# Attention means of two heads interleaved by 16 rows, fewer matmuls for v means and gate logits, and a new order of the work

## The chip, the cores and the metric

The kernel runs on one core of one Trainium2 chip. The metric is the device time of one execution in microseconds (us), as the median of several executions. A separate execution is recorded by the hardware profiler; it runs somewhat longer than the timed ones. PE is TensorE (PEld its weight loads), DVE is VectorE, ACT is ScalarE, POOL is GpSimd, SP issues DMAs.

## The reference, cut to what matters

Attention over 8 batches x 8 heads, 576 rows of 64, in two branches: a coarse one on means of 4 rows (144 x 144), repeated 4 times, and a local one over 7 neighbours. The sum, as 4608 rows of 512, goes through a top-1 mixture of 8 experts.

```python
q_d = q.reshape(B, H, Sd, 4, D).mean(axis=3)      # k_d, v_d alike; Sd = 144, D = 64
out_d = sm_attn(q_d, k_d, v_d)                    # softmax(q_d k_d^T / 8) v_d
out_up = np.repeat(out_d, 4, axis=2)
mask = np.abs(pos[:, None] - pos[None, :]) < 4
out_local = softmax(where(mask, q k^T / 8, -1e9)) @ v
attn_out = out_up + out_local                     # then x = (4608, 512)

logits = x @ w_gate                               # 8 experts
e_idx = np.argmax(logits, axis=1)
gate_w = softmax(logits)[e_idx];  eom = sigmoid(x @ w_output_gate)
out[mask_e] = gate_w * eom[:, e] * (relu(x[mask_e] @ w1[e]) @ w2[e])
```

## The kernel before

The work is cut into tasks, each on one engine with an assumed cost, a priority, inputs, and buffers that it takes and gives. A list scheduler inside the program orders them once, when the program is built; on the chip each engine runs its tasks in that fixed order. A unit `u` is one batch and two heads (32 units); heads 0 and 1 lie on partitions 0 to 63 and 64 to 127.

```python
def cast(u, i):                                   # i = 0: q, 1: k
    nc.gpsimd.tensor_copy(t16..., d["f", i])      # 96 x 768, f32 -> f16

def turn(u):                                      # 12 transposes into PSUM, tag "S"
    for i in range(2):
        for m in range(6):
            nc.tensor.transpose(tf[:, i, :]..., t16[:, m, :], id16[0:96, 0:96])

def turned(u):   nc.scalar.copy(d["qkT"]..., d["t"]...)
def qk_means(u): nc.vector.tensor_reduce(d["qkd"], d["qkT"]...(r=4), op=ALU.add)

def v_means(u):
    d["pd"] = pd = psA.tile([128, 2, 512], F32, tag="S", name="pd", bufs=3)
    for w in range(NW):                           # NW = 10 windows of 57 rows
        for h in range(2):
            j, c = (w // 2, 0) if w < 8 else (2 * h + 1, D)
            nc.tensor.matmul(pd[32 * j:32 * j + 32, h, c:c + D], lhsT=pv[64 * h:64 * h + 64, w, :],
                             rhs=d["v"][64 * h:64 * h + 64, w, 0:D], start=(w % 2 == 0), stop=(w % 2 == 1), ...)

def vd_out(u):                                    # three copies PSUM -> SBUF
    nc.scalar.copy(t[:, 0:2, 0:D], d["pd"][:, :, 0:D])
    for h in range(2):
        r = slice(64 * h + 32, 64 * h + 64)
        nc.scalar.copy(t[r, 2, 0:D], d["pd"][r, h, D:2 * D])

def scores(u):                                    # f16
    for g in range(2):                            # the mask is added by a matmul with the identity
        nc.tensor.matmul(ps[:, g, 0:NL], lhsT=id16, rhs=mk[:, g, :], start=True, stop=False, ...)
    for j in range(4):
        for h, r in hs:
            mm(ps[32 * j:32 * j + 32, h, MC:NH], kd[r, MW[2 * j]:MW[2 * j] + 32], qd[r])
    for w in range(NW):
        for h, r in hs:
            mm(ps[r, w // 5, LC[w]:LC[w] + QN[w]], d["qkT"][r, S + KW[w]:S + KW[w] + 64], qT[r, Q0[w]:Q0[w] + QN[w]])
    for g in range(2):
        for h, r in hs:
            mm(ps[r, g, TC:MC], kd[r, SD - 64:SD], qd[r, NK * g:NK * g + NK])

def exps(u):
    nc.scalar.activation(e[:, :, TC:NH], d["ps"][:, :, TC:NH], AF.Exp, scale=scale / 16.0)
    nc.scalar.activation(e[:, :, 0:TC], d["ps"][:, :, 0:TC], AF.Exp, scale=scale)

def values(u):                                    # f32
    for t in range(NB):                           # 5 blocks x 2 windows x 2 heads
        ... nc.tensor.matmul(po[h][64 * a:64 * a + 64, t, :], lhsT=e[r, w // 5, LC[w]:LC[w] + 64], rhs=t_v[r, w, 0:65], ...)
    for g in range(2):
        for h in range(2):
            nc.tensor.matmul(po[h][0:NK, NB + g, :], lhsT=e[:, h, MC + NK * g:MC + NK * g + NK], rhs=t_vd[:, h, 0:65], ...)
    for g in range(2):
        for h in range(2):
            r = slice(64 * h + 32, 64 * h + 64)
            nc.tensor.matmul(po[h][0:NK, NB + g, :], lhsT=e[r, g, TC:MC], rhs=t_vd[r, 2, 0:65], ...)
# ... norm (DVE), then per batch: upsample (PE), x_sum (DVE), x_high (ACT), x_low (POOL), x_turn (PE), x_turned ...

def logits(b, ts):                                # gate logits of one block of 128 rows
    for i, t in enumerate(ts):
        ms = [(xT[:, x + c, :], wg[:, c, y:y + 2 * E]) for x, y in ((0, 0), (0, 2 * E), (4, 0)) for c in range(4)]
        for j, (a, m) in enumerate(ms):
            nc.tensor.matmul(lg[:, i, :], lhsT=a, rhs=m, start=(j == 0), stop=(j == 11))

def logits_out(b, ts): nc.scalar.copy(lg_s[n][:, c:c + len(ts), :], lg[:, 0:len(ts)])

XT_ACT = (1, 3)                                   # blocks whose transposed copy is ACT's; the others are DVE's
# buffers: three large PSUM tiles "S" (tqk, pd, ps, po, pu, py), two small "T" (us, tp, lg, rk, ...)
```

After the routing come the experts: the rows of each are fetched, `up` (PE, pu) with a relu on ACT and DVE, `down` (PE, py), `weigh` (ACT) and `put` (an indirect DMA). Two experts begin early with the rows known by then.

Of the kernel before, what the change touches and what calls it, by code (L numbers as in the profile page):

```python
# [21 lines left out]
MW = [0, 15, 30, 44, 58, 72, 87, 101, 115, 129]  # L22
CW = [15, 15, 14, 14, 14, 15, 14, 14, 14, 15]
NW = 10
NB = 5
# [13 lines left out]
def kernel(  # L39
# [34 lines left out]

    NL = S // 2
# [4 lines left out]
    NH = MC + SD  # L80

    LT = MW[8] - (SD - 32)
    mk = cst.tile([128, 2, NL], F16)
    band = cst.tile([64, 2, 64], F16)
    pv = cst.tile([128, NW, 32], F32)
    nc.vector.memset(pv, 0.0)
    pb = cst.tile([64, 7, 16], F32)
# [23 lines left out]
    one = cst.tile([128, 2], F32)  # L111

    def make_means():


        nc.gpsimd.memset(pb, 0.25)
        select(pb, -1, [[-1, 7], [-4, 16]], 1)
        select(pb, 4, [[1, 7], [4, 16]], -1)
        nc.gpsimd.memset(one, 1.0 / XS)
        for j in range(4):  # L120
            select(one[32 * j:32 * j + 32, 0:1], CW[2 * j] + CW[2 * j + 1] - 1, [[0, 1]], -1)
            select(one[32 * j:32 * j + 32, 1:2], -LT, [[0, 1]], 1)

    def spread_means():
        for w in range(NW):
            c = CW[w - 1] * (w % 2) + LT * (w >= 8)
            nc.vector.tensor_copy(pv[0:64, w, c:c + CW[w]], pb[:, 4 * MW[w] - KW[w] - 1, 0:CW[w]])
        for x in vd_s:
            nc.vector.tensor_copy(x[:, 0:2, D], _ap(one, [one.ap[0], [0, 2]]))
            nc.vector.tensor_copy(x[:, 2, D:D + 1], one[:, 1:2])  # L130

    def spread_more():
        nc.scalar.copy(pv[64:128], pv[0:64])

    up_m = cst.tile([NK, 2, NW, 64], F16)
# [20 lines left out]
    slot_i = cst.tile([128, 1], I32)  # L156
    slot_f = cst.tile([128, 1], F32)
# [3 lines left out]
    def make_gate():  # L161
# [14 lines left out]
        nc.gpsimd.iota(slot_i, pattern=[[0, 1]], base=0, channel_multiplier=1)  # L176
# [8 lines left out]
    def gate_consts():  # L185
        for x in w9_s:
            nc.vector.tensor_copy(x[:, :, E], past)
        for o, x in ((rev, rev_i), (slot_f, slot_i)):
            nc.vector.tensor_copy(o, x)
        nc.vector.tensor_scalar_mul(wg[:, :, 0:2 * E], wgf, GS)  # L190
        nc.vector.scalar_tensor_tensor(wg[:, :, 2 * E:4 * E], in0=wgf, scalar=GS, in1=wg[:, :, 0:2 * E],
                                       op0=ALU.mult, op1=ALU.subtract)


    v_s, vd_s, xh_s = [], [], []
    for i in range(4):
        t_v = cst.tile([128, NW, D + 2], F32, tag=f"v{i}")
        nc.vector.memset(t_v[:, :, D:D + 2], 1.0 / XS)
        v_s.append(t_v)
        if i < 3:  # L200

            vd_s.append(cst.tile([128, 3, D + 2], F32, tag=f"vd{i}", name=f"vd{i}"))
        xh_s.append(cst.tile([128, NB, XW], F16, tag=f"xh{i}", name=f"xh{i}"))
    t_xl = cst.tile([128, NB, Dm], F16, tag="xl")
    cum = cst.tile([128, E], F16, tag="cum")
# [64 lines left out]
    def cast(u, i):  # L270
        d = st[u]
        d["s16", i] = t16 = sbA.tile([96, 6, 2, D], F16, tag=f"qk16{i}", name=f"qk16{i}")
        nc.gpsimd.tensor_copy(t16.rearrange("p m h d -> p h m d"), d["f", i])  # L273
# [17 lines left out]
    def qk_means(u):  # L291

        d = st[u]
        d["qkd"] = sbA.tile([128, 2 * SD], F16, tag="qkd", name="qkd", bufs=3)
        nc.vector.tensor_reduce(d["qkd"], d["qkT"].rearrange("x (n r) -> x n r", r=4), axis=AX.X, op=ALU.add)  # L295

    def v_means(u):

        d = st[u]
        d["pd"] = pd = psA.tile([128, 2, 512], F32, tag="S", name="pd", bufs=3)  # L300
        for w in range(NW):
            for h in range(2):
                j, c = (w // 2, 0) if w < 8 else (2 * h + 1, D)
                nc.tensor.matmul(pd[32 * j:32 * j + 32, h, c:c + D], lhsT=pv[64 * h:64 * h + 64, w, :],  # L304
                                 rhs=d["v"][64 * h:64 * h + 64, w, 0:D], start=(w % 2 == 0), stop=(w % 2 == 1),
                                 skip_group_check=True)

    def vd_out(u):
        d = st[u]
        d["vd"] = t = vd_s[u % 3]  # L310
        nc.scalar.copy(t[:, 0:2, 0:D], d["pd"][:, :, 0:D])
        for h in range(2):
            r = slice(64 * h + 32, 64 * h + 64)
            nc.scalar.copy(t[r, 2, 0:D], d["pd"][r, h, D:2 * D])

    def scores(u):


        d = st[u]
        qT = d["qkT"][:, 0:S]  # L320
        qd, kd = d["qkd"][:, 0:SD], d["qkd"][:, SD:2 * SD]
        d["ps"] = ps = psA.tile([128, 2, 512], F32, tag="S", name="ps", bufs=3)
        hs = [(h, slice(64 * h, 64 * h + 64)) for h in range(2)]
        mm = lambda o, a, m: nc.tensor.matmul(o, lhsT=a, rhs=m, start=False, stop=True, skip_group_check=True)  # L324
        for g in range(2):
            nc.tensor.matmul(ps[:, g, 0:NL], lhsT=id16, rhs=mk[:, g, :], start=True, stop=False,  # L326
                             skip_group_check=True)
        for j in range(4):
            for h, r in hs:
                mm(ps[32 * j:32 * j + 32, h, MC:NH], kd[r, MW[2 * j]:MW[2 * j] + 32], qd[r])  # L330
        for w in range(NW):
            for h, r in hs:
                mm(ps[r, w // 5, LC[w]:LC[w] + QN[w]], d["qkT"][r, S + KW[w]:S + KW[w] + 64],
                   qT[r, Q0[w]:Q0[w] + QN[w]])
        for g in range(2):
            for h, r in hs:
                mm(ps[r, g, TC:MC], kd[r, SD - 64:SD], qd[r, NK * g:NK * g + NK])

    def exps(u):

        d = st[u]
        d["e"] = e = sbA.tile([128, 2, NH], F32, tag="e", name="e")
        nc.scalar.activation(e[:, :, TC:NH], d["ps"][:, :, TC:NH], AF.Exp, scale=scale / 16.0)  # L343
        nc.scalar.activation(e[:, :, 0:TC], d["ps"][:, :, 0:TC], AF.Exp, scale=scale)

    def values(u):

        d = st[u]
        d["po"] = po2 = psA.tile([128, 2, 512], F32, tag="S", name="po", bufs=3)
        e, t_v, t_vd = d["e"], d["v"], d["vd"]  # L350
        po = [po2[:, h, 0:65 * (NB + 2)].rearrange("p (t c) -> p t c", c=65) for h in range(2)]


        for t in range(NB):
            for a in range(2):
                w = 2 * t + a
                for h in range(2):
                    r = slice(64 * h, 64 * h + 64)
                    nc.tensor.matmul(po[h][64 * a:64 * a + 64, t, :], lhsT=e[r, w // 5, LC[w]:LC[w] + 64],  # L359
                                     rhs=t_v[r, w, 0:65], start=(t == 0), stop=False, skip_group_check=True)  # L360
        for g in range(2):
            for h in range(2):
                nc.tensor.matmul(po[h][0:NK, NB + g, :], lhsT=e[:, h, MC + NK * g:MC + NK * g + NK],  # L363
                                 rhs=t_vd[:, h, 0:65], start=False, stop=False, skip_group_check=True)
        for g in range(2):
            for h in range(2):
                r = slice(64 * h + 32, 64 * h + 64)
                nc.tensor.matmul(po[h][0:NK, NB + g, :], lhsT=e[r, g, TC:MC], rhs=t_vd[r, 2, 0:65],  # L368
                                 start=False, stop=True, skip_group_check=True)

    def norm(u):
# [4 lines left out]
        po = d["po"][:, :, 0:65 * (NB + 2)].rearrange("p h (t c) -> p h t c", c=65)  # L376
        rs = sbA.tile([128, 2, NB + 2], F32, tag="rs")
        nc.vector.reciprocal(rs[:, :, 0:NB], po[:, :, 0:NB, 64])
        for h in range(2):
            c = D * (2 * hp + h)  # L380
            nc.vector.tensor_tensor(xo_s[b][:, 0:NB, c:c + D], po[:, h, 0:NB, 0:D], _bc(rs[:, h, 0:NB], D), op=ALU.mult)
        nc.vector.reciprocal(rs[0:NK, :, NB:], po[0:NK, :, NB:, 64])
        nc.vector.tensor_tensor(
            xo_s[b][0:NK, NB:, 2 * D * hp:2 * D * hp + 2 * D].rearrange("p t (h d) -> p h t d", h=2),
            po[0:NK, :, NB:, 0:D], _bc(rs[0:NK, :, NB:], D), op=ALU.mult)


    def xd_high(b):
        st["xdh", b] = x = sbA.tile([NK, 2, Dm], F16, tag="xdh", name="xdh", bufs=1)
        nc.scalar.copy(x, xo_s[b][0:NK, NB:NB + 2, :])  # L390

    def xd_low(b, g):
        if g == 0:
# [513 lines left out]
```

The softmax here doesn't subtract the row's maximum and nothing guards it: scores larger than these inputs give would overflow.

## Time and profile before

| | |
|---|---|
| time, median of 3 | 433.53 us (433.11 to 436.43) |
| span of the profiled execution | 448.3 us |
| mean granted TensorE clock | 0.867 |
| moved by DMA | 72.01 MB, mean 161 GB/s |
| chain that ended last, by engine | PE 74%, issue 12%, ACT, POOL and DVE 3% each, DMA 2% |
| longest waits of other engines | POOL put for ACT y 48.2 us; DVE norm for PE po 48.0 us |
| v means on PE (pd) | 1280 passes, 32.5 us busy |
| gate logits on PE (lg) | 480 matmuls, 15.8 us busy |

The profile gives, for each engine, busy time and its share of the span; a line of forty digits is the span in equal slices, in tenths of busy time or of full clock. A group line has the source line, engine, operation, tiles written and read, shape, count, then busy time and the mean of one, then the idle time of the engine before the group and what ended most of it. "issue" means that the profile shows nothing that the engine waited for. Ends of matmuls are modelled, so durations on PE are read from start to start.

### The profile page before, as it was taken

The numbers are of one execution on the slowest core, as the hardware profiler recorded it, in microseconds if no ns is written. First come the engines' busy times: TensorE is split into PE (matmuls) and PEld (weight loads), VectorE is DVE, ScalarE is ACT, GpSimd is POOL, SyncE is SP. The second block draws the span as 40 slices with busy tenths as digits, with TensorE's granted clock in tenths as the row PEclk, the third lists the DMA queues.
The fourth block names the chain that finished last, engine by engine and source line by source line (L and its number), as shares of the span: only waits on it lengthen the run. The fifth ranks groups of instructions, "written<-read, shape, count | busy, mean of one in ns | idle before, by whom it ended". The sixth has DMA issues, their size and how long they took to land.

```text
span 448.3 us, 14930 instructions
## 1 busy us (share of the span) xinstructions
PE 389.8 (87%) x6479; PEld 273.3 (61%) x6479; DVE 203.9 (45%) x478; ACT 200.6 (45%) x400; POOL 227.8 (51%) x278
## 2 busy tenths in 40 slices
PE   3887988988978989889879978797999999999990
PEld 2665667776657777677656645454766565665640
DVE  5435356565664667548436368431523231322300
ACT  4517357474444756554635244232344243342521
POOL 7644355583761969556825365353353435042151
PEclk9959669899597999878955576899999999999996
DMA  9999979796562796993281013117799999781121
GB/s 219 225 289 278 323 206 217 142 220 134 155 174 54 193 212 130 219 232 77 85 139 33 12 45 105 53 66 271 152 208 282 205 227 202 177 163 57 63 111 70
DMA packets 76948, 72.01 MB, mean 161 GB/s; under 512 B 46478, under 2 KB 67022, under 8 KB 76872
## 3 DMA queue, kind: packets, MB, share of 16 engines
q1 hardware_dynamic: 58952, 39.97, 35.9%
q0 software_dynamic: 17920, 30.98, 32.3%
q8 instruction: 53, 0.87, 0.8%
q14 instruction: 23, 0.19, 0.1%
HBM read 68.23 MB, written 21.05 MB: 199 GB/s over the span
## 4 chain that ended last, share of the span: by engine, by line
PE 74%; issue 12%; ACT 3%; POOL 3%; DVE 3%; DMA 2%; another core or an unknown queue 1%; POOLq 0%; ACTq 0%; DVEq 0%
PE pu L593 13%; PE py L616 10%; PE po L359 7%; PE us L402 6%; PE pd L304 6%; PE po L363 6%; PE ps L324 6%; PE tqk L282 4%; PE po L368 3%; PE tp L417 3%; PE lg L437 3%; PE ps L326 3%; PE tp L419 2%; DMA out_dram<-y,xh 2%; PE gtp L565 2%
## 5 line engine op out<-in xcount | busy, mean ns | idle before, releaser
L593 PE MATMUL pu<-xgT,w1sb 128*128 128x384 f16 (+1 forms) x512 | 72.8, 303 | 0.7 <-DVE xgT L576 0.3
L628 POOL DMA_INDIRECT out_dram<-y,xh x40 | 40.1, 1002 | 54.6 <-ACT y L624 48.2
L273 POOL CAST qk<-qk 96x768 f16<-96x768 f32 x64 | 51.3, 824 | 30.6 <-issue 18.4
L593 PEld LDWEIGHTS <-w1sb 128*128 128x128 f16 x512 | 50.5, 99 | 22.2 <-issue 2.5
L616 PE MATMUL py<-w2sb,hs 128*128 128x512 f16 x272 | 60.8, 379 | 0.0
L412 POOL TENSOR_TENSOR t_xl<-xo,xh 128x512 f16<-128x512 f32 x38 | 43.9, 1169 | 31.6 <-ACT xh L409 28.2
L608 DVE TENSOR_SCALAR hs<-pu 128x256 f16<-128x256 f32 x56 | 23.8, 425 | 68.0 <-ACT hs L606 33.3
L624 ACT ACTIVATE y<-py,xh 128x512 f32<-128x512 f32 x40 | 26.0, 685 | 58.0 <-PE py L616 41.1
L523 POOL DMA_INDIRECT hx_xs<-xh,pos x40 | 40.0, 999 | 22.1 <-DVE more L825 8.5
L295 DVE TENSOR_REDUCE qkd<-qkT 128x288 f16<-128x1152 f16 x32 | 42.7, 1344 | 15.0 <-ACT qkT L288 14.9
L616 PEld LDWEIGHTS <-hs 128*128 128x128 f16 x272 | 26.1, 98 | 29.2
L304 PE MATMUL pd<-t_v,pv 64*32 64x64 f32 x1280 | 32.5, 256 | 10.9 <-issue 10.0
L288 ACT COPY qkT<-tqk 128x1152 f16<-128x1152 f16 x32 | 35.7, 1122 | 13.2 <-PE tqk L282 13.0
L359 PE MATMUL po<-t_v,e 64*64 64x65 f32 x1280 | 34.4, 257 | 8.0 <-issue 6.0
L606 ACT ACTIVATE hs<-pu 128x384 f16<-128x384 f32 (+1 forms) x56 | 26.4, 475 | 27.8 <-PE pu L593 23.9
L395 POOL TENSOR_TENSOR xdl<-xo,xdh 72x512 f16<-72x512 f32 x15 | 17.0, 1149 | 41.5 <-ACT xdh L390 41.5
L343 ACT ACTIVATE e<-ps 128x432 f32<-128x432 f32 x32 | 17.1, 533 | 46.2 <-PE ps L324 21.7
L359 PEld LDWEIGHTS po<-t_v,e 64*64 64x64 f32 x1280 | 28.5, 164 | 14.5 <-issue 7.1
L406 DVE TENSOR_TENSOR xo<-us,xo 128x512 f32<-128x512 f32 x40 | 26.6, 685 | 19.5 <-PE us L402 16.8
L304 PEld LDWEIGHTS pd<-t_v,pv 64*32 64x32 f32 x1280 | 25.0, 126 | 16.8 <-issue 13.1
L282 PE MATMUL tqk<-id,qk 96*128 96x96 f16 x384 | 26.7, 226 | 8.0 <-POOL qk L273 6.1
L409 ACT CAST xh<-xo 128x512 f16<-128x512 f32 x40 | 24.3, 619 | 14.5 <-DVE xo L406 12.8
(122 smaller groups left out, 618.1 us busy)
## 6 DMA issues: line engine op xcount, KB each, us to landing
t_v<-in_v_dram SPq DMA_DIRECT2D x63, 160.0 KB
qk<-in_q_dram SPq DMA_DIRECT2D x32, 288.0 KB
qk<-in_k_dram SPq DMA_DIRECT2D x32, 288.0 KB
w1sb<-in_moe_w_dram POOLq DMA_DIRECT2D x16, 512.0 KB
w2sb<-in_moe_w_dram POOLq DMA_DIRECT2D x16, 512.0 KB
hx_xs<-zt SPq DMA_DIRECT2D x8, 645.0 KB
xh<-hx_xs SPq DMA_DIRECT2D x6, 645.0 KB
xh<-hx_xs SPq DMA_DIRECT2D x2, 387.0 KB
```

The costliest lines, as they stand in the source:

```text
L273: nc.gpsimd.tensor_copy(t16.rearrange("p m h d -> p h m d"), d["f", i])
L282: nc.tensor.transpose(tf[:, i, :].bitcast(F16)[:, 96 * m:96 * m + 96], t16[:, m, :], id16[0:96, 0:96])
L288: nc.scalar.copy(d["qkT"].rearrange("x (i p m) -> x i p m", i=2, m=6), d["t"].bitcast(F16)[:, :, 0:S].rearrange("x i (m p) -> x i p m", m=6))
L295: nc.vector.tensor_reduce(d["qkd"], d["qkT"].rearrange("x (n r) -> x n r", r=4), axis=AX.X, op=ALU.add)
L304: nc.tensor.matmul(pd[32 * j:32 * j + 32, h, c:c + D], lhsT=pv[64 * h:64 * h + 64, w, :], rhs=d["v"][64 * h:64 * h + 64, w, 0:D], start=(w ...
L324: mm = lambda o, a, m: nc.tensor.matmul(o, lhsT=a, rhs=m, start=False, stop=True, skip_group_check=True)
L359: nc.tensor.matmul(po[h][64 * a:64 * a + 64, t, :], lhsT=e[r, w // 5, LC[w]:LC[w] + 64], rhs=t_v[r, w, 0:65], start=(t == 0), stop=False, ...
L412: (nc.vector if b == B - 1 and t % 2 else nc.gpsimd).tensor_tensor(t_xl[:, t], xo_s[b][:, t, :], xh_s[b % 4][:, t, 0:Dm], op=ALU.subtract)
L523: ins = nc.gpsimd.indirect_dma_start(out=xs_dram.ap(), out_offset=bass.IndirectOffsetOnAxis(ap=gs[n]["pos"][:, c:c + 1], axis=0), in_=xh_s ...
L593: nc.tensor.matmul(ps[:, i, 0:x.shape[2]], lhsT=wts[e][0][:, c, 128 * f:128 * f + 128], rhs=x[:, c, :], start=(c == 0), stop=(c == 3))
L616: nc.tensor.matmul(ps[:, i, :], lhsT=d["hs"][:, f, c:c + 128], rhs=wts[e][1][:, f, :], start=(f == 0), stop=(f == NG - 1))
L628: ins = nc.gpsimd.indirect_dma_start(out=out, out_offset=bass.IndirectOffsetOnAxis(ap=d["xg"][:, j, Dm // 2 + 1:Dm // 2 + 2], axis=0), in_ ...
```

## The change

It aims at fewer and wider PE instructions. Rows of the means are interleaved by head, 16 of one and 16 of the other, so that one matmul over all 128 partitions serves both heads: v means take 6 matmuls instead of 20. For the coarse logits, the key means are spread into block-diagonal form (zeros for the other head), so that one matmul with 128 rows gives both heads; the values of the coarse branch come for both heads side by side (130 columns). The factor 1/16 moves into the key spread, so one exponential serves all logits. Gate logits of one block take 8 matmuls: the high half of x meets high and low weights side by side (32 columns), and the two sums are added by DVE on the way out. Some k casts, one more transposed copy per batch and the second half of the key spread go to ACT, the logit copies to DVE. v means move to the small PSUM tiles. All priorities are new, and the scheduler now tracks which very buffer comes free next.

```diff
+    pv = cst.tile([128, 4, 2, 16], F32)
 ...
 def cast(u, i):
-        nc.gpsimd.tensor_copy(t16.rearrange("p m h d -> p h m d"), d["f", i])
+        (nc.scalar.copy if i * (u % 2) else nc.gpsimd.tensor_copy)(t16.rearrange("p m h d -> p h m d"), d["f", i])
 ...
+    def k_means(u, h):
+        qd, kd = st[u]["qkd"]
+        x = qd[64 * h:64 * h + 64, SD:SD + 16]
+        o, x = kd[64 * h:64 * h + 64, :, :, h, :], _ap(x, [x.ap[0], [57, 3], [14, 4], [1, 16]])
+        if h:
+            nc.scalar.activation(o, x, AF.Copy, scale=1.0 / 16.0)
+        else:
+            nc.vector.tensor_scalar_mul(o, x, 1.0 / 16.0)
 def v_means(u):
-        d["pd"] = pd = psA.tile([128, 2, 512], F32, tag="S", name="pd", bufs=3)
-        for w in range(NW): ...                   # 20 matmuls, as above
+        d["pd"] = pd = psA.tile([128, 3, D], F32, tag="T", name="pd", bufs=2)
+        mm = lambda j, o, c, m: nc.tensor.matmul(pd[32 * j:32 * j + 32, o], lhsT=pv[:, c].rearrange("p h i -> p (h i)"),
+                                                 rhs=m, start=True, stop=True, skip_group_check=True)
+        for j in range(4):
+            w = d["v"][:, j, 0:D]
+            n = 3 if j < 2 else 2
+            mm(j, slice(0, n), j, _ap(w, [w.ap[0], [4 * (D + 2), n], w.ap[1]]))
+        for j in range(2, 4):
+            mm(j, 2, j - 2, d["v"][:, 6 + j, 0:D])
 def vd_out(u):
-        nc.scalar.copy(t[:, 0:2, 0:D], d["pd"][:, :, 0:D])   # and two smaller ones
+        for h in range(2):
+            nc.scalar.activation(t[:, :, h, 0:D], d["pd"], AF.Copy, scale=head[:, h:h + 1])
 def scores(u):
         for g in range(2):
-            nc.tensor.matmul(ps[:, g, 0:NL], lhsT=id16, rhs=mk[:, g, :], ...)
-        for j in range(4):
-            for h, r in hs:
-                mm(ps[32 * j:32 * j + 32, h, MC:NH], kd[r, MW[2 * j]:MW[2 * j] + 32], qd[r])
+            n = (NL, MC)[g]
+            nc.tensor.matmul(ps[:, g, 0:n], lhsT=id16, rhs=mk[:, g, 0:n], ...)
         ...                                       # the 20 windows stay
         for g in range(2):
-            for h, r in hs:
-                mm(ps[r, g, TC:MC], kd[r, SD - 64:SD], qd[r, NK * g:NK * g + NK])
+            mm(ps[64 * g:64 * g + 64, 0, TC:MC], kd[:, 2, 0:2].rearrange("p j h i -> p (j h i)"),
+               qd[:, NK * g:NK * g + NK])
+        for i in range(2):
+            mm(ps[:, i, MC:NH], kd[:, i].rearrange("p j h i -> p (j h i)"), qd)
 def exps(u):
-        ...                                       # two activations
+        nc.scalar.activation(e, d["ps"][:, :, 0:NH], AF.Exp, scale=scale)
 def values(u):
         ...                                       # the 20 windows stay
-                nc.tensor.matmul(po[h][0:NK, NB + g, :], lhsT=e[:, h, ...], rhs=t_vd[:, h, 0:65], ...)     # x4
-                nc.tensor.matmul(po[h][0:NK, NB + g, :], lhsT=e[r, g, TC:MC], rhs=t_vd[r, 2, 0:65], ...)   # x4
+                mm(g, e[:, i, MC + NK * g:MC + NK * g + NK], t_vd[:, i], False)                            # x4, 130 columns
+            mm(g, e[r, 0, TC:MC], t_vd[r, 2], True)                                                        # x2, r = 64 rows
 def logits(b, ts):
-            for j, (a, m) in enumerate(ms): ...   # 12
+            for c in range(8):
+                n = (4 if c < 4 else 2) * E
+                nc.tensor.matmul(lg[:, i, 0:n], lhsT=xT[:, c, :], rhs=wg[:, c % 4, 0:n], start=(c == 0), stop=(c == 7), ...)
 def logits_out(b, ts):
-        nc.scalar.copy(...)
+        nc.vector.tensor_reduce(lg_s[n][:, c:c + len(ts), :], lg...rearrange("p t (a e) -> p t e a", a=2), axis=AX.X, op=ALU.add)
-    XT_ACT = (1, 3)
+    XT_ACT = (1, 2, 3)
-    LEAN = {...}                                  # all priorities
+    LEAN = {...}
 ...
     def schedule():
-        room = dict(ROOM)                         # counts of free buffers
+        taken, given = {r: [] for r in ROOM}, set()
+        gives = {key: owners(key) for key in tasks}
+        can = lambda r: len(taken[r]) < ROOM[r] or (taken[r][-ROOM[r]], r) in given
```

Left out here: the set-up of the constants (the mean matrices are built by fewer steps, row sums come from three small matmuls once), the halves of the upsampled means padded to 128 rows with zeros, and dependencies of tasks that follow from the above.

## The prediction

> **What bounds the kernel now.** I read the page first, then the busy time by stage, then the order of time on PE in a stretch at full clock, then PE's idle gaps. The page:
>
> ```profile
> span 448.3 us, 14930 instructions
> PE 389.8 (87%) x6479; PEld 273.3 (61%) x6479; DVE 203.9 (45%) x478; ACT 200.6 (45%) x400; POOL 227.8 (51%) x278
> PE   3887988988978989889879978797999999999990
> PEclk9959669899597999878955576899999999999996
> q8 instruction: 53, 0.87, 0.8%
> ```
>
> PE is busy for 87% of the span and no other engine passes 51%. The slices show two halves. From slice 27 on PE is full at full clock: these are the experts, which the change leaves alone. Before that PE has small holes, and its clock keeps falling to half. The sums by stage (PE, PEld, DVE, ACT, POOL, clock, DMA share, GB/s):
>
> ```profile
> 8.00:288.00 280.00, 242.31 (x5498) 184.11 (x5496) 158.64 (x351) 141.53 (x289) 160.75 (x188) 0.80 0.70 161
> 288.00:441.00 153.00, 145.80 (x970) 87.97 (x968) 41.50 (x100) 55.97 (x106) 60.33 (x65) 1.00 0.70 163
> ```
>
> In 8 to 288 us (attention, 32 pairs of heads) the mean clock is 0.80. The clock is recorded only as 1 or 0.5, so 40% of the stage, 112 us, ran at half. The experts cannot start before the last rows are routed, so what this stage gains moves the end by as much. The order of time for one pair of heads at full clock (start, us, then the group):
>
> ```profile
> 144.21 0.74 PE L304 MATMUL pd<-t_v,pv 64*32 64x64 f32 x40
> 144.88 0.42 PE L326 MATMUL ps<-mk,id 128*128 128x288 f16 x2
> 145.23 0.26 PE L324 MATMUL ps<-qkd 64*32 64x144 f16 x8
> 145.41 0.51 PE L324 MATMUL ps<-qkT 64*64 64x60 f16 x20
> 145.75 0.23 PE L324 MATMUL ps<-qkd 64*64 64x72 f16 x4
> 145.87 0.81 PE L359 MATMUL po<-t_v,e 64*64 64x65 f32 x40
> 146.62 0.73 PE L363 MATMUL po<-vd,e 128*72 128x65 f32 x8
> 147.28 0.47 PE L368 MATMUL po<-vd,e 32*72 32x65 f32 x8
> 147.68 0.42 PE L326 MATMUL ps<-mk,id 128*128 128x288 f16 x2
> ```
>
> From start to start: v means 0.67, logits of attention 0.99, values 1.81 (0.75 + 0.66 + 0.40); the transposes (tqk) add 0.56. That is 4.03 us per pair, 129 us for 32. The batch work at full clock adds 96 upsampling matmuls x 0.215, 320 transposes x 0.056 and the gate logits (480 x 0.028 = 13.6), together 52. So about 181 us of full-clock PE work takes 280 us. The rest is half clock, holes, and some early expert work at the end of the stage. A hole:
>
> ```profile
> 17.32 0.41 PE L304 MATMUL pd<-t_v,pv 64*32 64x64 f32 x10
> 19.70 0.69 PE L304 MATMUL pd<-t_v,pv 64*32 64x64 f32 x30 [1.97 <-issue]
> ```
>
> One group of 40 stops after 10 passes for 1.97 us, and nothing that the profile shows released it. Instruction packets: 0.87 MB in 53 is 16.4 KB each[...]. I numbered the PE records in the trace. Thirteen holes of 0.5 to 2.3 us, 17.1 us together, all between 8 and 288 us, sit at record 193 or 194 of a run of 256, and end 1.2 to 1.6 us after an instruction packet landed. PE has used its block of instructions before the next one is there. From one crossing to the use of the next block the fetch needs 3.5 to 7 us here, and in this stage a block lasts 6.3 us on average. Most half-clock stretches begin within 4 us of such a hole.
>
> [...]
>
> **The change, PE.** An fp32 matmul is two passes[...].
> - v means: 40 passes become 12[...]. Saves 0.15.
> - attention logits: eight 64x32 matmuls go (-0.18). The second mask is 72 columns longer (+0.03). The four small ones (0.12) become two 128x64 and two 128x128 ones of 144 columns[...]. Net +0.18, less some overlap: I take +0.12.
> - values: the 20 windows stay. The four block matmuls move 130 columns instead of 65[...]: 0.69 for 0.66. The last four become two on 64 rows: 0.30 for 0.40. Saves 0.07.
> - together -0.10 per pair, 3.2 us for 32. Gate logits: 480 become 320 at 28 ns, -4.5 us. At the stage's mean clock the sum is about -9 us.
>
> **Instructions of PE.** Passes per pair: 12+40+34+56 = 142 become 12+12+26+52 = 102; per batch 12+40+60 = 112 become 92. Two instructions each: 10,880 become 8,000, so 11 of some 42 blocks of the stage go, and a block lasts about 8 us instead of 6.3. I expect the holes to fall from 17 us to about 5. The profiled run is 15 us longer than the timed median (448.3 against 433.5), so the timed run may have smaller holes: I count -8. Half clock costs 112 us x 0.87 busy x 0.39 = 38 us (groups take 1.6 to 1.75 times as long there: values windows 1.29 against 0.74). With fewer holes a third of it should go: -12.
>
> **The other engines.** ACT has, on the page and in its groups:
>
> ```profile
> L344 ACT ACTIVATE e<-ps 128x576 f32<-128x576 f32 x32 | 20.7, 647 | 0.0
> L343 ACT ACTIVATE e<-ps 128x432 f32<-128x432 f32 x32 | 17.1, 533 | 46.2 <-PE ps L324 21.7 <-PE po L368 20.6 <-PE lg L437 3.9
> ```
>
> These give 0.79 ns a column and 0.19 fixed, so one exponential of 1008 columns takes 0.99 instead of 1.18: -6. Added: 16 casts of k (768 columns, about 0.83: +13), the third transposed block per batch (8 x 1.01: +8), a key spread (192 columns, 0.35 x 32: +11). The v-mean copies stay near 0.7, the logit copies leave (-4.5). ACT goes up by 22 us, to about 164 in a stage of 255: 64%. DVE: -5.5 for the 8 blocks, +8 for the key spread, +5 for the logit sums. POOL: -13. Beside PE these lie in the shade, but ACT holds two steps that PE waits for in every pair (the qk copy and the exponential), and the key spread puts 0.4 us between means and logits. For this and for the new order I add +8. v means leave the three large PSUM buffers for the two small ones, which eases the former.
>
> Sum: 433.5 - 9 - 8 - 12 + 8 = 412.5.
>
> **Rivals.**
> 1. ACT becomes what PE waits for. For: it waits 41 us for PE on po and ps, so the loop is tight, and it gets 22 us more. Against: 64% is far from full. Then only the pure PE saving is left or less: 424 to 433.
> 2. Wider full-row fp32 matmuls cost more than the load: if a pass streamed at two cycles per column, or the column tiles did not overlap with 128 rows, v means would take 0.9 to 1.0 and values 2.0, +0.5 us a pair, +16: about 425. Against: 64-column passes at 64x32 already start 27 ns apart, one cycle a column.
> 3. The order decides. All priorities are new, and the planner now tracks which buffer comes free. A good order leaves PE waiting nowhere and the clock up: 395 to 402. A bad one gives 440. The traces of before can't tell.
> 4. Holes are in the profiled run only: then the fetch and half of the clock gain go, about 420.
>
> **Range and chances.** The PE part is small and sure, the holes and the clock are large and uncertain, the order goes both ways. 398 to 430. Faster by over 2% (below 424.9) 0.79, within 0.14, slower 0.07.
>
> **What would show it.** Instruction packets down to about 42. v means near 0.52 us a group at full clock, attention logits 1.1, values 1.74. Holes at block boundaries below 7 us. Clock in the attention stage at 0.86 or more. The attention stage ends 18 to 30 us earlier, the experts' 153 us unchanged. ACT near 222 us busy. I am wrong if PE's groups are as I say but its idle time before ps and po, ended by ACT, grows; or if the clock stays at 0.80 with the holes gone.

## Result, and the profile after

The changed kernel took 402.32 us (median of 4, 399.64 to 404.48), beside 434.98 us (433.11 to 437.96) for the kernel before: ratio 0.924, 95% interval 0.9153 to 0.9328. The prediction was 412.5 us, range 398 to 430. In a second comparison with fresh executions of both it was 401.86 us, ratio 0.925 (0.9174 to 0.9327). The ratios leave out the slow executions and the medians do not, so the two can differ.

The head of the page of after (span; busy time of each engine; slices of PE and of its clock; the queue of instruction packets):

```profile
span 397.9 us, 12048 instructions
PE 354.9 (89%) x5045; PEld 243.4 (61%) x5045; DVE 216.6 (54%) x535; ACT 225.5 (57%) x367; POOL 215.2 (54%) x262
PE   3879888898999998989998679989999999999980
PEclk9999999998999999999999869999999999999995
q8 instruction: 41, 0.67, 0.8%
```

PE is as full as it was (89% after 87%), and no other engine has come near it. What differs is the row of the clock: before it had fives and sixes all through the first 26 slices, now it is nine in all but four. To compare the attention stage alone, take the stretch from 8 us to about the last matmul of the values, first before (columns: stretch, length, busy time of PE, PEld, DVE, ACT, POOL, clock, DMA share, GB/s):

```profile
8.00:258.00 250.00, 220.13 (x5212) 169.26 (x5209) 139.29 (x300) 130.80 (x268) 142.62 (x171) 0.81 0.76 171
```

and after:

```profile
8.00:213.00 205.00, 188.00 (x3844) 140.17 (x3841) 149.35 (x345) 155.37 (x241) 130.22 (x154) 0.99 0.96 209
```

The stretch is 45 us shorter. Of this 32 us are busy time of PE and 13 us idle time. From the last gate logits to the end, before took 166.5 us and after 164.4: the experts didn't gain. (The profiled execution of before took some 15 us more than its timed ones, while that of after is one of the timed, so the 45 us overstate what the medians show, which is 33.)

PE's work for one pair of heads at full clock, in the order of time (start, us, then the group; durations are read from start to start):

```profile
111.79 0.44 PE L353 MATMUL ps<-mk,id 128*128 128x288 f16 x2
112.16 0.51 PE L350 MATMUL ps<-qkT 64*64 64x60 f16 x20
112.60 0.46 PE L350 MATMUL ps<-t_qd,t_kd 128*64 128x72 f16 x4
112.89 0.55 PE L460 MATMUL lg<-wg,xT 128*128 128x32 f16 x16
113.37 0.54 PE L329 MATMUL pd<-t_v,pv 128*32 128x192 f32 x12
113.84 0.68 PE L300 MATMUL tqk<-id,qk 96*128 96x96 f16 x12
...
115.36 0.81 PE L383 MATMUL po<-t_v,e 64*64 64x65 f32 x40
116.10 1.49 PE L385 MATMUL po<-vd,e 128*72 128x130 f32 x12
117.52 0.36 PE L460 MATMUL lg<-wg,xT 128*128 128x32 f16 x8
```

Attention logits 111.79 to 112.89: 1.10. v means 113.37 to 113.84: 0.47. Values 115.36 to 117.52: 2.16, of which the windows are 0.74 and the twelve 130-column passes 1.42. Eight gate logits take 0.2 us. With the transposes (0.53) a pair costs 4.26 us, against 4.03 before: +0.23, or +7.4 us for 32 pairs. The gate logits give back 4.6 us (480 x 0.028 less 320 x 0.0275). **So at full clock PE has not less but some 3 us more to do, in fewer and larger instructions.** So the 32 us of PE's busy time must be half-clock time that went away.

What PE waits for, before (8 to 281 us: the time in total, how often, and the longest), its largest entries:

```profile
PE pd L304 <- issue: 10.0, 10, 2.1
PE po L359 <- issue: 6.0, 5, 2.3
PE ps L324 <- issue: 2.7, 2, 1.4
```

and after (8 to 233 us):

```profile
PE lg L460 <- DVE xT L451: 3.4, 4, 1.1
PE us L424 <- ACT vd L342: 2.4, 4, 0.9
PE us L424 <- DVE xo L429: 2.2, 4, 1.1
PE po L383 <- ACT e L369: 2.1, 3, 1.2
```

The waits without a releaser have left the head of the list, and small waits for other engines have come. I sorted PE's holes over 0.25 us by the PE record at which they begin. At the ends of blocks of 256 records (in before these holes stand at record 193 or 194 of each 256): 17.1 us in 13 before, 4.3 us in 8 after (2.0 us of these have a releaser, and may fall there by chance). Elsewhere without a releaser: 9.8 us before, none after. Elsewhere with a releaser: 7.3 us before, 16.9 after.

### The profile page after: what moved, and what is told of

Same layout as the page of the kernel before. It is cut to its first block, busy times and chain, and to the rows that moved or that the text cites. A ratio compares the mean times of both kernels' runs of the same rounds, so it can differ in the third digit from the quotient of the medians.

```text
span 397.9 us, 12048 instructions
## 1 busy us (share of the span) xinstructions
PE 354.9 (89%) x5045; PEld 243.4 (61%) x5045; DVE 216.6 (54%) x535; ACT 225.5 (57%) x367; POOL 215.2 (54%) x262
## 4 chain that ended last, share of the span: by engine, by line
PE 60%; DVE 11%; ACT 8%; issue 8%; DMA 5%; POOL 5%; POOLq 0%; SPq 0%; DVEq 0%; ACTq 0%
PE pu L618 15%; PE py L641 13%; PE po L385 9%; PE po L383 5%; PE ps L350 4%; PE us L424 3%; DMA w1sb<-in_moe_w_dram 3%; PE tqk L300 3%; DVE xo L429 2%; PE gtp L590 2%; ACT qkT L306 2%; DVE t_qd L313 2%; PE tp L440 2%; POOL out_dram L653 2%; ACT vd L342 2%
## 5 line engine op out<-in xcount | busy, mean ns | idle before, releaser
L291 POOL CAST qk<-qk 96x768 f16<-96x768 f32 x48 | 38.9, 828 | 22.0 <-PE tqk L300 6.4
L385 PE MATMUL po<-vd,e 128*72 128x130 f32 (+1 forms) x384 | 49.6, 293 | 0.9 <-ACT vd L342 0.7
L313 DVE TENSOR_REDUCE t_qd<-qkT 128x288 f16<-128x1152 f16 x32 | 43.1, 1346 | 10.7 <-ACT qkT L306 10.5
L369 ACT ACTIVATE e<-ps 128x1008 f32<-128x1008 f32 x32 | 32.3, 1011 | 16.9 <-PE ps L350 13.9
L385 PEld LDWEIGHTS po<-vd,e 128*72 128x72 f32 (+1 forms) x384 | 36.2, 145 | 9.1 <-issue 6.0
L383 PE MATMUL po<-t_v,e 64*64 64x65 f32 x1280 | 27.4, 229 | 3.4 <-ACT e L369 2.1
L405 DVE TENSOR_TENSOR xo<-po,rs 128x320 f32<-128x320 f32 x64 | 28.4, 486 | 1.5
L449 ACT COPY xT<-tp 128x1024 f16<-128x1024 f16 x24 | 23.9, 1014 | 8.8 <-PE tp L442 8.7
```

What stands on the lines that cost most here:

```text
L291: (nc.scalar.copy if i * (u % 2) else nc.gpsimd.tensor_copy)(t16.rearrange("p m h d -> p h m d"), d["f", i])
L313: nc.vector.tensor_reduce(d["qkd"][0][:, 0:2 * SD], d["qkT"].rearrange("x (n r) -> x n r", r=4), axis=AX.X, op=ALU.add)
L369: nc.scalar.activation(e, d["ps"][:, :, 0:NH], AF.Exp, scale=scale)
L383: nc.tensor.matmul(po[64 * a:64 * a + 64, h, 65 * t:65 * t + 65], lhsT=e[r, w // 5, LC[w]:LC[w] + 64], rhs=t_v[r, w, 0:65], start=(t == 0) ...
L385: mm = lambda g, a, m, z: nc.tensor.matmul(po[0:NK, g, PM:PM + 130], lhsT=a, rhs=m.rearrange("p h d -> p (h d)"), start=False, stop=z, ski ...
```

## The experiments

The theories, which the expectations call by these names or describe:

- **WORK**: the time follows PE's work at full clock.
- **FETCH**: PE stands still at the ends of instruction blocks, and the clock falls because of that; fewer instructions cure both.
- **ACTIVITY**: the clock follows how much of the array is in use. The instructions of after use more rows and columns at once, partly on zeros, and hold the clock up themselves.
- **ORDER**: the new priorities do it.

Times are compared within one group of runs only. Beside the four runs from "more instructions" on, before took 456.16 us; beside the next four, 435.61; beside the last four, 438.25. For the last four and for one of the second group there is no ratio. Why before is 20 us slower beside the first of these groups no trace here shows, so that group's stages and holes are only roughly comparable with the other rows. "Stage" is the stretch from 8 us to the last windows of the values, in the profiled execution; holes are PE's, over 0.25 us, from 8 us to the last gate logits. The clock is the one that the profile gives for the stage. It counts what comes before the first record of the clock as full, though PE runs at half pace there (12 transposes take 1.07 us, not 0.53): up to 14.7 us in before, 24.6 with padded rows, 29.6 with half of the v means.

| run | time, us | beside it, before | ratio (95%) | stage, us | clock in it | block holes, us | other holes, us | packets |
|---|---|---|---|---|---|---|---|---|
| before (first profile) | 434.98 | | | 250.8 | 0.81 | 17.1 | 17.1 | 53 |
| after | 402.32 | 434.98 | 0.924 (0.915-0.933) | 205.1 | 0.99 | 4.3 | 16.9 | 41 |
| more instructions | 464.06 | 456.16 | 1.018 (1.008-1.029) | 270.4 | 0.92 | 19.1 | 23.3 | 54 |
| after, plain order | 453.81 | 456.16 | 1.005 (0.999-1.010) | 248.8 | 0.92 | 5.9 | 45.4 | 41 |
| before, plain order | 474.86 | 456.16 | 1.032 (1.018-1.045) | 267.8 | 0.79 | 21.6 | 30.2 | 53 |
| before, half of v means | 576.92 | 456.16 | not comparable | 262.6 | 0.75 | 14.3 | 14.1 | 49 |
| before, padded rows | 425.29 | 435.61 | 0.983 (0.976-0.990) | 231.3 | 0.90 | 24.4 | 8.9 | 53 |
| the same, padded masks | 430.49 | 435.61 | | 238.8 | 0.90 | 28.3 | 10.6 | 53 |
| after, again | 401.86 | 435.61 | 0.925 (0.917-0.933) | 205.6 | 0.99 | 3.4 | 15.4 | 41 |
| after, 72 rows | 405.52 | 435.61 | 0.935 (0.928-0.942) | 208.4 | 0.98 | 3.9 | 14.2 | 41 |
| after, fp16 coarse | 403.56 | 438.25 | | 202.5 | 0.95 | 8.1 | 26.7 | 40 |
| after, other order | 406.74 | 438.25 | | 212.3 | 0.98 | 6.7 | 18.7 | 41 |
| fp16 and other order | 403.87 | 438.25 | | 209.2 | 0.92 | 10.9 | 27.3 | 40 |
| before, gate logits alone | 432.87 | 438.25 | | 246.1 | 0.81 | 22.8 | 9.4 | 51 |

### More instructions in after

```diff
-            mm(j, slice(0, n), j, ...)                 # v means: 6 matmuls of 64 to 192 columns
+            for o in range(n):
+                for c in range(2): mm2(j, o, j, c, ...)    # 20 + 4 of 32 columns
-        mm(g, a, m)                                    # coarse values: 6 of 130 columns
+        for h in range(2): ...                         # 12 of 65
-            mm(ps[:, i, MC:NH], ..., qd)               # block-diagonal logits: 144 columns
+            for c in range(2): ...                     # 2 x 72
```

> The kernel after, in its own order, with its PE work cut into more instructions that move the same columns: v means in 24 matmuls of 32 columns (48 passes for 12), the coarse values in 65 columns for 130 (24 passes for 12), the two block-diagonal logits in 72 columns for 144. PE instructions of the attention stage go from 8,000 to about 11,300, more than the 10,900 of before. Theory FETCH (fewer instructions, so fewer holes while PE waits for its next block, so the clock stays up): packets back to about 54, holes of 10 us and more, mean clock of the stage 0.88 or less, 420 to 432 us. Theory ORDER (the new order keeps PE fed): clock 0.95 or more, at most 408. Theory ACTIVITY (matmuls on all 128 rows count as more activity for the clock): holes return, clock stays at 0.95, about 412.

It took 464.06 us, 1.018 of before. The order of time on PE (one group broken by a hole, then values at full clock):

```profile
110.03 0.56 PE L389 MATMUL po<-t_v,e 64*64 64x65 f32 x21
114.00 0.56 PE L389 MATMUL po<-t_v,e 64*64 64x65 f32 x19 [3.41 <-issue]
...
121.28 0.81 PE L389 MATMUL po<-t_v,e 64*64 64x65 f32 x40
122.02 1.67 PE L393 MATMUL po<-vd,e 128*72 128x65 f32 x24
```

With after's arithmetic and before's number of instructions (54 packets), the block holes are back at 19.1 us, up to 3.4 us each. But the clock in the stage is 0.92, not before's 0.81, so the holes alone don't make before's clock: FETCH had 0.88 or less. ACTIVITY, which had it stay at 0.95, fails too, and whether it fell from 0.99 by the holes or by the narrower passes this run can't tell. Nor is it a clean test of the cost of the holes: the v means now take 1.21 us for 0.47 (48 passes of 32 columns, one every 25 ns) and the coarse values 1.60 for 1.42, so PE has about 0.9 us a pair more to do, 29 us in all. If after had run at 0.924 of before here, at 421 us (it wasn't among these runs), the remaining 13 us or so would be what the holes and the lower clock cost together. That is an estimate; the prediction counted 8 and 12 us for the two.

### Both kernels with all priorities at the plain order

```diff
-    LEAN = {"ahead": 21.75, "band": -8.95, ...}
+    LEAN = {}                                          # in before and in after, each by itself
```

> The work of the kernel after without its tuned priorities: every task keeps only the natural priority of its unit. FETCH: 41 packets, few holes, clock 0.92 or more, at most 418 us. ORDER: the gain goes with the priorities, 428 or more.

> The work of the kernel before without its tuned priorities, the pair to the run above. FETCH: 53 packets and holes as in before, 430 to 450 us, so over 20 us slower than the same natural order of the work after. ORDER: the two natural orders lie within 10 us of each other.

After with a plain order: 453.81 us. Before with a plain order: 474.86 us. The slices of PE's clock on the page, of after with the plain order:

```profile
PEclk9997798999699999699999677998998899999997
```

and of before with the plain order:

```profile
PEclk9875568995855998969989555799999799999996
```

With the order taken out of both, the rest of the change is worth 21 us of medians (4.4%; the fastest executions, 448.62 and 467.85, differ by 19). PE's idle time is nearly the same in the two (51 and 52 us of holes), but the clock isn't: 0.92 against 0.79. In before the tuned order is worth 19 us (474.86 to 456.16), in after about 32 (453.81 to the estimate of 421). So ORDER carries a part that the prediction had only as its third rival: without its tuned order the changed kernel is no faster than the kernel before with one. The old priorities in the new kernel, or the new ones in the old, weren't tried.

### Before with half of its v means

```diff
-            for h in range(2):
+            for h in range(1):                         # means of the even head, used for both
```

> The kernel before with v means of the even head only (the odd head gets the same means; its own are left out): 20 passes for 40, on the same column tiles side by side, so PE's time for them hardly falls (0.67 to 0.6 a unit, 2 us in all), while 1,280 of its 10,900 instructions of the stage go. Order and everything else as before. FETCH: 48 packets, holes fall from 17 us to 10 or less, clock of the stage up from 0.80 to 0.86 or more, 420 to 428 us. ORDER and ACTIVITY: 430 to 433.

The odd heads get the even heads' v means here, so other rows go to other experts; expert 1 overflows its 640 rows (computed from the reference, it has 637, and 657 with these means), and a loop at the end, which otherwise has nothing to do, runs for some 130 us. The total of 576.92 us says nothing; the attention stage can be read. The slices of its page, PE and clock:

```profile
PE   5989989898988979798788999999997004000000
PEclk9985766856999868656689999999999556555555
```

640 passes fewer, and the block holes fall to 14.3 us, yet the clock of the stage is 0.75, not 0.86 or more as FETCH has it, and the stage is 12 us *longer* than in the first profile of before. But the profiled execution took 587.39 us, where the other four took 574 to 578, and it stands beside a profile from another comparison. So I take from it only that no gain in clock was seen; that the clock fell isn't shown.

### Zero rows in before's upsampling

Looking for another way in which before and after differ, I found one that the prediction passes over: after runs the upsampling matmuls on 128 rows, of which 56 are zero, and before on 72. Alone, in before:

```diff
-    up_m = cst.tile([NK, 2, NW, 64], F16)
+    up_m = cst.tile([128, 2, NW, 64], F16)
+    xd_s = {x: cst.tile([128, 2, Dm], F16, ...)}       # zero once; only rows 0 to 71 are written
```

> The kernel before with its upsampling matmuls on 128 rows instead of 72 (the added rows are zeros on both sides): same instructions, same columns, same order, same result. Theory ACTIVITY (the clock follows how much of the array is in use, counted as columns moved x rows x weight columns, zeros included; over the windows of the traces so far the border between staying at full clock and falling to half lies at about a third of the array): use in the stage rises by 0.03 to 0.04, mean clock of the stage up by 0.03 or more, 4 to 10 us faster than before. Theory FETCH (only the holes from instruction fetch bring the clock down): nothing changes, within 2 us.

The clock and the instruction queue on its page, then the sums of its stage:

```profile
PEclk9998699699699986899996995999999999999996
...
q8 instruction: 53, 0.87, 0.9%
```

```profile
8.00:239.00 231.00, 202.87 (x5241) 158.46 (x5243) 138.39 (x301) 130.72 (x270) 142.70 (x171) 0.90 0.84 185
```

The same instructions, as many packets, as many columns moved, with nothing but zeros added; the clock of the stage rises from 0.81 to 0.90 (from 30 us on, 0.81 to 0.89; that of the whole span, in the timed executions, from a median of 0.873 to 0.915, and the two sets don't overlap) and the time falls by 1.7% (10 us of medians). FETCH can't explain this: the block holes *grew*, from 17 to 24 us, and all holes together stayed as they were (34.2 and 33.3 us). That a faster PE made them grow isn't shown: the run with the gate logits alone, below, has 22.8 us of them at before's clock. What this run shows is a part of ACTIVITY: rows in use raise the clock, even when they hold zeros.

### Zero columns in the masks on top of that

```diff
-            nc.tensor.matmul(ps[:, g, 0:NL], lhsT=id16, rhs=mk[:, g, :], ...)     # 288 columns
+            nc.tensor.matmul(ps[:, g, 0:NH], lhsT=id16, rhs=mk[:, g, :], ...)     # 504, zeros
```

> As the run above, and the two mask matmuls of each unit move 504 columns instead of 288 (zeros added where the coarse logits follow): 432 columns of pure ballast a unit on the full array, 0.18 us, 5.8 us of more PE work in all, no further instructions. ACTIVITY: mean clock up by 0.06 or more over before, at least as fast as the run above although PE does more, 6 to 14 us faster than before. FETCH: 3 to 6 us slower than before.

430.49 us (423.99 to 436.63; with padded rows alone 423.40 to 428.98), clock 0.90 again. The masks cost 5.8 us more of PE's time (0.53 for 0.35 a pair), and no more clock came of it. ACTIVITY had expected a time no longer than with padded rows alone; the spread leaves open whether it is longer. So more work on the full array isn't shown to help wherever it is put.

### After once more, and after with upsampling on 72 rows

```diff
-            nc.tensor.matmul(ps, lhsT=up_m[:, g, ...], rhs=xd_s[x][:, g, :], ...)
+            nc.tensor.matmul(ps, lhsT=up_m[0:NK, g, ...], rhs=xd_s[x][0:NK, g, :], ...)
```

> The kernel after, unchanged, beside the kernel before on this chip, for comparison with the other runs of this call: ratio 0.92 by both theories.

> The kernel after with its upsampling matmuls on 72 rows as in before. ACTIVITY: use in the stage lies well above the border already (0.41 and more in 95% of the windows that stayed at full clock), so the clock falls by 0.02 at most and the time rises by 0 to 4 us. FETCH: no change, within 2 us.

Taking the padding out of after costs 3.7 us (405.52 against 401.86; clock 0.98 against 0.99). That is less than the 7 to 10 us which it brings in before: after holds its clock by more than this padding.

### Fp16 for the coarse values, and another order

```diff
-        d["e"] = e = sbA.tile([128, 2, NH], F32, ...);  nc.scalar.activation(e, d["ps"][:, :, 0:NH], AF.Exp, ...)
+        d["ec"] = ec = sbA.tile([128, 2, NH - TC], F16, ...)
+        nc.scalar.activation(ec, d["ps"][:, :, TC:NH], AF.Exp, ...)
+        d["e"] = e = sbA.tile([128, 2, NL + 8], F32, ...);  nc.scalar.activation(e, d["ps"][:, :, 0:NL + 8], ...)
-        mm(g, e[:, i, MC + ...], t_vd[:, i], False)
+        mm(g, ec[:, i, NK + ...], t_vd[:, i], False)   # t_vd in F16 too
```

> The changed kernel, with the coarse logits' exponentials and the block means of v in fp16 and not fp32, so that the six 130-column matmuls of the values are fp16; one exponential becomes two (fp32 for the windows, fp16 for the rest). Everything else, priorities too, as after. If an fp32 matmul costs two cycles a column and the fp16 one a single cycle, the six matmuls take about 0.5 us in place of 1.42 a unit, and PE has some 29 us less to do. WORK theory (time follows PE's work): stage clock stays at 0.97 to 0.99, the last values come some 15 to 25 us earlier, 378 to 390 us. ACTIVITY theory (the clock follows the share of the array in use): the same matmuls count half as much, the stage's clock falls to 0.80 to 0.92, and most of the saving is lost: 392 to 405 us. In either case ACT is busy some 6 us longer, and packets on the instruction queue stay at 41.

> The changed kernel with another set of priorities (found by replaying orders with the durations that the trace of after shows, in which it came out 0.5 us shorter), nothing else changed. If the order of after is at its best already, 400 to 405 us; if orders near it differ by as much as the tuned and the plain one do (30 us), anything to 415. The clock should stay above 0.96 in the stage, since the work is the same.

> The fp16 coarse matmuls with the other set of priorities. WORK: 378 to 390 us. ACTIVITY: 392 to 405 us, with a stage clock of 0.80 to 0.92. Against the run with fp16 alone it shows how much of that run's time is its order.

With fp16: 403.56 us, against 402.32 and 401.86 for after in its own comparisons. The order of time, then the stage:

```profile
127.37 0.81 PE L385 MATMUL po<-t_v,e 64*64 64x65 f32 x40
128.11 0.60 PE L387 MATMUL po<-vd,ec 128*72 128x130 f16 x6
128.64 0.39 PE L426 MATMUL us<-xdh,up_m 128*128 128x512 f16 x1
```

```profile
8.00:210.00 202.00, 171.73 (x3636) 123.06 (x3636) 148.36 (x344) 155.72 (x272) 128.81 (x153) 0.95 1.00 212
```

The coarse matmuls take 0.53 us (128.11 to 128.64) in place of 1.42, about the 0.5 expected. At full clock that would be 28 us less for 32 pairs; PE's busy time in the stage fell by 16 only, in part because the clock fell to 0.95, and PE's holes grew from 21 to 35 us, so that the last values come 2.6 us earlier and the end doesn't move. WORK fails again. ACTIVITY has the time right, but the clock fell less than it said (0.80 to 0.92): the larger part of what was lost went into waits, and into holes at block ends (8.1 us for 4.3). After itself did not run beside this group. The closest pair within it is the other order, 406.74 us, and the same with fp16, 403.87: 3 us for 28 us less work, with the clock of the stage at 0.98 and 0.92.

### The 8-matmul gate logits alone, in before

```diff
-                nc.tensor.matmul(lg[:, i, :], lhsT=a, rhs=m, ...)                 # 12 per block, 16 columns
+                nc.tensor.matmul(lg[:, i, 0:n], lhsT=xT[:, c, :], rhs=wg[:, c % 4, 0:n], ...)    # 8
-        nc.scalar.copy(lg_s[n]..., lg)
+        nc.vector.tensor_reduce(lg_s[n]..., lg..."p t (a e) -> p t e a", op=ALU.add)
```

> The kernel before with the gate logits of a token block in 8 matmuls and not 12, and the sum of the two halves in a reduction on DVE, alone. It saves 160 small matmuls (25 ns each at full clock, 4.1 us; more at half clock) and one or two instruction packets (packets 52). WORK: about 4 to 5 us off, 430 us. ACTIVITY: these are passes of 16 columns, which use little of the array, so taking them away leaves denser work in the windows after a head group: clock of the stage 0.80 to 0.83, 428 to 432 us. If the gain of the change lay here, it would be more than 8 us.

432.87 us beside 438.25, clock 0.81 as before. The difference is about what was expected, but it lies inside the spread of before (426.65 to 444.52), so all it says is that the gain of the change isn't mainly here.

### A count over the windows of the clock

In the traces I took each window of 3.41 us that ran at full clock, and asked whether the next still did. Over a window I summed the columns moved (twice for each pass of fp32: the 130-column passes of after start 110 to 115 ns apart, those of the run in fp16 56 to 61), times the share of the 128 rows, times the share of the 128 weight columns, over 8192. That is about what fits: the 512-column fp16 passes start 216 ns apart at full clock, which would make 8090 columns in 3.413 us. Beside it, the same sum without rows and columns:

```
                     array use: stays (lowest 5%)  falls (highest)   columns alone: stays (lowest 5%)  falls (highest)
before                          0.366                  0.329                           0.767               1.177
before, padded rows             0.344                  0.312                           0.752               0.923
after                           0.411                  0.359                           0.709               0.359
after, fp16 coarse              0.394                  0.360                           0.662               0.855
```

The use of the array separates the windows nearly: those below about a third to 0.36 fall, those above stay, and a few lie on the wrong side. Columns alone don't separate them in three of the four kernels. But PE's idle time, which lowers the use too, separates them about as well, so this count doesn't decide between ACTIVITY and FETCH: up to the last gate logits of before, each of the 11 windows after which the clock falls has 1.0 to 2.3 us of holes, and those after which it stays have 0.93 at most. Nor is idle time a clean border: with padded rows a window with 0.77 us of it (use 0.232) falls, and one with 1.70 (use 0.395) stays. What idle time does not explain is how long the clock stays down. In before, 11 falls bring 32 windows at half clock, and in 11 of the 21 after which it stayed at half PE had no hole at all; with padded rows 7 falls bring 16 windows, in after 3 falls bring 3. This reading is fitted to these traces; that padding with zeros raises the clock is the part that a run shows.

## Why the prediction was right, and where it wasn't

The time fell in the range, 10 us below the middle. Several steps were wrong and made up for each other: PE's work came out 12 us dearer than predicted and half clock 17 us cheaper, so that the sum lay in the range is in part luck.

| step | predicted | measured |
|---|---|---|
| v means, full clock | 0.52 | 0.47 |
| attention logits | 1.11 | 1.10 |
| values | 1.74 | 2.16 |
| PE's work in all | -9 us | about +3 us |
| instruction packets | 42 | 41 |
| holes at block ends | 17 to 5 us | 17.1 to 4.3 us |
| holes without a releaser elsewhere | none named | 9.8 to 0 us |
| waits for other engines | +8, with the order | +9.6 us |
| half clock | -12 us | about -29 us |
| ACT busy | 222 us | 225.5 us |
| experts | unchanged | 2 us shorter |

The predicted 0.52, 1.11 and 1.74 are the author's estimates; before has no fp32 pass of more than 65 columns from which to read what a wider one costs.

- **Values: wrong.** The step priced the block matmuls at 0.69 us with 130 columns for 0.66 with 65: a wider pass was to cost nearly nothing more. That was the author's estimate, and nothing in before shows it. The group of block matmuls is now 12 passes (six fp32 matmuls) in 1.42 us, one every 118 ns; within a burst the starts are 110 to 115 ns apart. In before such passes of 65 columns start 65 ns apart, so 65 more columns cost 45 to 50 ns a pass. The spacing is twice the 0.42 ns a column of the 512-column fp16 passes (216 ns each; 2 x 130 x 0.42 = 109); in fp16 passes of 130 columns start 56 to 61 ns apart. What sets the 65 ns of the narrower fp32 passes isn't shown. The prediction took 0.42 ns a column from the 27 ns between 64x32 passes, and that was no evidence: those passes stand on different parts of the array and run beside each other (they start 7 and 20 ns apart by turns, and a group moves 40 x 64 columns in 0.67 us, 0.26 ns a column), so the interval says nothing of one pass. Rival 2 had this term (values 2.0), but expected the v means to be hurt as well (0.9 to 1.0), and they came out at 0.47: their passes are on four column tiles and overlap (12 passes with 1536 columns in all, 0.31 ns a column; in the group at 113.37 they start two by two, 6 to 10 ns apart).
- **Half clock: the right mechanism for a part, and much too small.** The mean clock of the whole span in the timed executions was 0.873 before (median of 11) and 0.970 in after, run beside it. Half-clock time is 2 x (1 - clock) x time: 111 us and 24 us. By the prediction's own 0.34 us for each of them the 87 us are worth 29 us. The prediction took a third of before's half clock off, for fewer holes. That holes bring the clock down fits the traces (all 11 falls of before), but it had no term for the share of the array in use, of which the padded run shows the rows; how much of the 29 us is due to either is open. It had the upsampling on 128 rows before it in the diff and passed over it as no work, and it counted the zeros of the block-diagonal means as a price alone.
- **Holes: right.** The packets (41 for 42), the place of the holes and their remainder (4.3 us for 5) came as worked out. Over all these runs 3.4 to 28.3 us of holes stood at block ends.
- **ACT and rival 1:** ACT got 25 us where 22 were counted, and did not become the bound. The waits for other engines grew by 9.6 us, close to the +8.
- **Rivals 3 and 4:** rival 3 named 395 to 402 for a good order that leaves the clock up, and the result stands at that edge. Order matters (19 and 32 us), but at the plain order the clock of after is above before's all the same (0.92 against 0.79). Rival 4 fell: the timed executions gained 33 us.

For rival 1, the group of the merged exponential in after:

```profile
L369 ACT ACTIVATE e<-ps 128x1008 f32<-128x1008 f32 x32 | 32.3, 1011 | 16.9 <-PE ps L350 13.9
```

One takes 1.011 us where 0.99 was worked out, and it waits 13.9 us for PE's logits, while PE waits 2.1 us for it: ACT follows PE, not the other way round.

With the measured terms, from the profiled executions except for the clock: +3 of work, -13 of holes at block ends and -10 of other holes without a releaser, +10 of waits, -29 of half clock are -39 us; 33 were measured. The profiled execution of before ran 15 us longer than its timed ones, so the -23 may be too much for them; the holes of the timed executions aren't recorded. How the 33 us divide between array use, fewer instructions and order stays open: each changes the others' terms (in the padded run the block holes grew while the clock rose), and no run here has after's number of instructions with before's use of the array.

## What to carry to other kernels

Before counting instructions on PE, count what share of the array they fill in each window of a few microseconds: where the clock stays at half with PE busy, filling up rows, even with zeros, can be worth more than taking work away (here 1.7% from zeros alone, and no more than 3 us from 28 us less work in fp16). Read the cost of a wide fp32 pass from passes that follow each other on the same part of the array, not from passes that lie side by side (here 110 to 115 ns for 130 columns, where 27 ns between 64-column passes would give 55). And when one engine issues thousands of small instructions, look for holes without a releaser at a fixed distance in its record numbers (here 256, and 17.1 us in 13 holes).

## What the runs showed that I had not expected

- With more rows in use the clock of PE rose, though they held zeros: 0.81 to 0.90 in the stage from 56 rows of zeros in 96 matmuls. The clock is recorded as 1 or 0.5, and its stretches in before and after are multiples of 3.41 us but for the last. What counts for it besides rows the runs don't settle; a PE without a hole was not enough for full clock in 11 windows of before.
- Fp32 passes of 130 columns that follow each other on the same tile start 110 to 115 ns apart, twice the 0.42 ns a column of the 512-column fp16 passes. The six matmuls in fp16 took 0.53 us for 1.42.
- Holes at block ends differ much between runs with nearly the same instructions: 17.1 us at a clock of 0.81 and 24.4 and 28.3 at 0.90, with 53 packets each, but also 22.8 at 0.81 with 51. By the numbering of its records, where a hole followed in before, the next instruction packet began 1.8 to 4.8 us after PE entered the block and had landed 1.2 to 1.6 us before PE went on.
